# A pooled attention with a squared-ReLU network behind it, on one core: another order of the front, one key pair and three small steps moved

## The chip, the cores and the metric

The kernel runs on one core of a Trainium2 chip. The metric is the device time of one execution in microseconds. The core has a matrix engine (TensorE, "PE" in the profile), a vector engine (VectorE, "DVE"), an activation engine (ScalarE, "ACT"), a general engine (GpSimd, "POOL") and SyncE ("SP"), which here issues most of the transfers. Each engine has its own queue of instructions and works through it in order; engines wait for one another by semaphores.

## The reference

Eight batches of eight heads with 576 positions and 64 features per head; keys and values are averaged over groups of eight positions, which leaves 72 of each. The result of the attention, with the heads put side by side, is 4608 tokens of 512 features, and goes through a network of two weights with a squared ReLU between them. Everything is float32.

```python
k_p = k.reshape(B, H, Sp, 8, D).mean(axis=3)
v_p = v.reshape(B, H, Sp, 8, D).mean(axis=3)
scores = scale * np.matmul(q, k_p.transpose(0, 1, 3, 2))
scores = scores - np.max(scores, axis=-1, keepdims=True)
attn = np.exp(scores)
attn = attn / (np.sum(attn, axis=-1, keepdims=True) + 1e-09)
x = np.matmul(attn, v_p)           # -> (4608 tokens, 512), heads side by side
h = np.maximum(x @ w_in, 0.0)      # 512 -> 2048
out = h * h @ w_out                # 2048 -> 512
```

## The kernel before, in words

**Tiling.** The 4608 tokens go through in nine chunks of 512. A chunk has 16 steps, one for each block of 128 hidden features: a step computes one hidden block (`h_n`, products of the chunk's four tiles `x_0` to `x_3`, one for each pair of heads, with the first weights `wf_i`), and, three steps later (`LAG`), that block's share of the output (`o_0` to `o_3`, which stay in PSUM for the whole chunk). Step numbers in the code run on over the chunks: chunk 2's first step is 32. Between the two come the ReLU and the square on ScalarE (`r_n`). In the first two chunks (`PLAIN = 2`) the products are plain; from chunk 2 on the hidden blocks are made of seven products of halves instead of eight, from sums and differences of weights that VectorE and ScalarE prepare (`wf_i`, `w_S`) and of tokens, and the second product is split in a high and a low part (`gh`, `gl`).

**Attention.** It is made for the chunk ahead while the network of the current chunk runs. In chunks 0 and 1 a pair of heads goes through `token_scores` (products `sps` of queries `st` and keys `kf`, then on VectorE the two maxima `tm`, as minima of the negated scores, and on ScalarE eight exponentials `te`, four for each head), `token_normalise` (VectorE: a sum, a small product, a reciprocal, a product over all of `te`), `token_turn` (TensorE transposes into `pps`, copied to `sc`) and `weigh_values` (`av`, copied to `x_p`). From chunk 2 on the scores are transposed; `exponents` subtracts the maxima from `sc` on VectorE, takes exponentials on ScalarE and sums on GpSimd with an all-reduce over the partitions (`tot`, and `mx` for the maxima before it); `transpose_q` transposes the queries on VectorE (`qs`) and splits them in high and low parts `st` on ScalarE and VectorE. Keys and values of a batch are summed over their eight positions: batch 0's first three key pairs on VectorE (`reduce_k`, two reduces into `kq`), its fourth pair, its values, and batch 1's keys and values on GpSimd (`halve_k`, `halve_v`: three adds of halves each). TensorE turns the sums (`turn_k`, transposes into `kps`), ScalarE copies them to `kf`. `late_turn_k` is `turn_k` with its copy at once.

**Weights.** They are converted on the chip from their words: `magnitude` (ScalarE, two instructions for a weight tile) and `to_float32` (VectorE, three: a clamp and two combinations of bits). In the first chunk this is VectorE's main work.

**Products of zeros.** `keep_awake(c, t, n)` puts `n` products of a tile of zeros (`still`) in TensorE's queue, in chunk 0 only. `STIR` of them stand at the very start (`stir`), `STAY` behind the second pair's queries and keys (`stay`), and `AWAKE` ahead of each `token_scores`, `token_turn` and `weigh_values`.

**PSUM.** `o_0` to `o_3` have a buffer each; `h` has two; and the pool `ps_a` with the tag `a` has two, which `kps`, `pps` and, in chunk 1, `sps` go through in turn.

**What sets the order.** Every instruction is recorded through `InOrder` and stays in program order on its engine, so the listing of an engine is the order of the code; all of them have one line in the profile (L34). The front is written out by hand (lines 729 to 794). After it, `at(step, f, ...)` puts a function on a step, and the loop at the end goes through the steps. The functions in `on_pe` put their products between a step's hidden block and its output products; `late_turn_k` is not among these and runs behind the output products, at the head of the step's other work. `STEADY` and `EARLY` hold the steps of the attention's functions, relative to a pair's first step; the attention of chunk 3 (`PLAIN + 1`) begins beside chunk 1 and goes on in chunk 2's steps, 32 and up.

## Time and profile before

| | us |
|---|---|
| median of 3 runs (lowest, highest) | 910.28 (909.4, 911.02) |
| the profiled execution's own time | 910.27 |
| its span, from the first to the last instruction | 908.5 |
| TensorE busy | 894.3 (98%) |
| VectorE busy | 568.1 (63%) |
| ScalarE busy | 509.6 (56%) |
| GpSimd busy | 421.1 (46%) |

A row of a timeline reads: start in the span, duration, engine, line, operation, the tile written and the tiles read, the shapes, how many instructions it stands for, and in brackets the idle time ahead of it on this engine with what ended it. Where a row stands for several instructions, the duration is that of all together. Rows of TensorE have modelled ends, so neighbours may overlap a little. A list of waits gives the total, how many times and the longest. The granted clock of TensorE was 0.999 over this execution.

### The profile page before, as it was taken

What the parts mean: (1) busy time and instruction counts of PE and PEld (TensorE: products, weight loads), DVE (VectorE), ACT (ScalarE), POOL (GpSimd) and SP (SyncE); (2) the same over time, 40 slices, a digit from 0 to 9 for tenths busy, and PEclk for the clock granted to TensorE, in tenths of its full rate; (3) what the DMA queues carried; (4) which work ended last, traced back from release to release, by engine and by line L of the source; (5) the groups of instructions that cost most, each with busy time, mean ns of one, the idle gap of its engine ahead of it and who ended that gap; (6) DMA issues with size and microseconds to landing.
All of it is one profiled execution on the core that took longest, in us unless ns stands there. A gap on an engine that the chain in (4) does not pass through costs nothing.

```text
span 908.5 us, 14140 instructions
## 1 busy us (share of the span) xinstructions
PE 894.3 (98%) x5090; PEld 715.2 (79%) x5093; DVE 568.1 (63%) x946; ACT 509.6 (56%) x1017; POOL 421.1 (46%) x227
## 2 busy tenths in 40 slices
PE   8999999999999999999999999999999999999998
PEld 5444445777878888888888888888888888889987
DVE  7997778668688877456755575648544653353222
ACT  5866756656565656554655556455644564344442
POOL 3753245566555456566555655564444444200000
PEclk9999999999999999999999999999999999999999
DMA  9898574877555666665575556654533353245401
GB/s 222 263 261 189 140 177 110 229 227 196 130 155 141 143 143 142 178 156 118 133 207 135 120 143 179 153 132 117 170 109 113 105 164 116 96 173 197 175 1 47
DMA packets 157335, 138.72 MB, mean 153 GB/s; under 512 B 94488, under 2 KB 122136, under 8 KB 157264
## 3 DMA queue, kind: packets, MB, share of 16 engines
q1 hardware_dynamic: 128464, 127.13, 46.5%
q0 software_dynamic: 28800, 10.68, 10.3%
q8 instruction: 40, 0.66, 0.3%
q14 instruction: 31, 0.25, 0.1%
HBM read 119.65 MB, written 18.06 MB: 152 GB/s over the span
## 4 chain that ended last, share of the span: by engine, by line
PE 82%; DMA 6%; DVE 4%; ACT 2%; POOL 2%; issue 2%; SPq 1%; DVEq 0%; ACTq 0%; POOLq 0%
PE o L34 40%; PE h L34 35%; PE av L34 3%; PE sps L34 3%; SPq L34 1%; DMA rb<-rd 1%; POOL k L34 1%; DMA k<-in_k_dram 1%; DMA v<-in_v_dram 1%; DMA w_o<-kept 1%; DVE gl L34 1%; DVE wf_i L34 1%; DMA rd<-rr 1%; ACT sc L34 0%; DVE xf L34 0%
## 5 line engine op out<-in xcount | busy, mean ns | idle before, releaser
L34 PE MATMUL o<-w_o,gh 128*128 128x512 f32 x1024 | 322.3, 396 | 2.0 <-DMA w_o<-kept 2.0
L34 POOL PARTITION_ALL_REDUCE tot<-sc x56 | 187.8, 3403 | 86.4 <-issue 86.4
L34 PEld LDWEIGHTS o<-w_o,gh 128*128 128x128 f32 x1024 | 184.3, 188 | 46.8 <-issue 6.6
L34 PE MATMUL o<-w_o,gl 128*128 128x512 f32 x512 | 200.9, 392 | 0.0
L34 ACT ACTIVATE r<-h 128x512 f32<-128x512 f32 x144 | 83.6, 595 | 94.4 <-PE h L34 74.2
L34 PE MATMUL h<-x_T,w_S 128*128 128x256 f32 x1008 | 130.2, 283 | 0.5 <-ACT r L34 0.5
L34 POOL PARTITION_ALL_REDUCE mx<-sc x56 | 112.4, 2048 | 37.0 <-ACT sc L34 25.9
L34 PEld LDWEIGHTS h<-x_T,w_S 128*128 128x128 f32 x1008 | 124.9, 191 | 0.7 <-ACT r L34 0.7
L34 PEld LDWEIGHTS o<-w_o,gl 128*128 128x128 f32 x512 | 96.2, 188 | 21.3 <-DVE gl L34 0.4
L34 DVE TENSOR_TENSOR h<-h,u 128x256 f32<-128x256 f32 x168 | 72.6, 432 | 64.1 <-ACT u L34 33.7
L34 ACT COPY u<-h 128x256 f32<-128x256 f32 x112 | 41.8, 373 | 115.2 <-PE h L34 70.8
L34 PE MATMUL h<-x_B,w_A 128*128 128x256 f32 x672 | 98.6, 283 | 0.5 <-ACT r L34 0.5
L34 PEld LDWEIGHTS h<-x_B,w_A 128*128 128x128 f32 x672 | 91.6, 189 | 5.6 <-ACT r L34 1.1
L34 DVE TENSOR_TENSOR gl<-r,gh 128x512 fp32r<-128x512 f32 x128 | 92.1, 755 | 5.4 <-ACT gh L34 5.3
L34 POOL DMA_DIRECT2D k<-in_k_dram x36 | 44.1, 1225 | 109.1 <-issue 60.4
L34 POOL DMA_DIRECT2D v<-in_v_dram x36 | 44.1, 1224 | 107.4 <-issue 50.3
L34 DVE TENSOR_TENSOR u<-h,u 128x256 f32<-128x256 f32 x56 | 23.4, 417 | 101.9 <-ACT u L34 101.8
L34 ACT ACTIVATE r<-r 128x512 f32<-128x512 f32 x144 | 84.2, 625 | 1.1
L34 DVE TENSOR_TENSOR st<-qs,st 64x512 fp32r<-64x512 f32 x56 | 45.1, 806 | 61.8 <-ACT st L34 61.0
L34 ACT CAST gh<-r 128x512 fp32r<-128x512 f32 x128 | 78.9, 616 | 0.6 <-PE o L34 0.4
L34 ACT ACTIVATE sc<-sc 72x512 f32<-72x512 f32 x56 | 34.5, 632 | 69.3 <-DVE sc L34 69.3
L34 PE MATMUL h<-x,wf_i 128*128 128x512 f32 x128 | 57.8, 595 | 0.8 <-ACT x L34 0.8
(96 smaller groups left out, 1213.0 us busy)
## 6 DMA issues: line engine op xcount, KB each, us to landing
w_o<-kept SPq DMA_DIRECT2D x128, 512.0 KB
out_dram<-ob SPq DMA_DIRECT2D x36, 256.0 KB
raw_i<-in_moe_w_in_dram SPq DMA_DIRECT2D x16, 512.0 KB
raw_o<-in_moe_w_out_dram SPq DMA_DIRECT2D x16, 512.0 KB
kept<-w_o SPq DMA_DIRECT2D x16, 512.0 KB
rb<-rd SPq DMA_DIRECT2D x56, 128.0 KB
k<-in_k_dram POOLq DMA_DIRECT2D x36, 144.0 KB, 5.1
v<-in_v_dram POOLq DMA_DIRECT2D x36, 144.0 KB, 5.0
```

Of the source, the lines that this page charges most:

```text
L34: return lambda *a, **k: self.tc.keep_in_program_order(f(*a, **k))
```

## The change

1. **Fewer products of zeros.** `STAY` is 5 in place of 7 and `AWAKE` is (1, 1, 0) in place of (3, 2, 0): 2, 8 and 4 products less, 14 in all. The `stay` products now stand behind the second pair's scores and write to the pool `ps_a`.
2. **The third key pair of batch 0** is summed on GpSimd with three adds, no longer on VectorE with two reduces.
3. **The front in another order.** `token_scores` of chunk 0 gives its maxima and its exponentials as two functions, which the front calls apart. The normalisations and turns of pairs 0 and 1 come earlier. The second three conversions of the first weight tile, on VectorE, stand ahead of the normalisation of pair 3 (they stood behind it).
4. **Batch 1's keys.** `late_turn_k` takes a list of pairs: the first three stay in step 3, the fourth goes to step 4.
5. **Chunk 3.** `exponents` of its pair 1 and `transpose_q` of its pair 2 come one step later, 33 for 32.

TensorE, steps 3 to 5 of chunk 0, before (`kps`: transposes of batch 1's key sums; `sps_0`: scores of chunk 1's first pair; what stands in brackets are the engines whose semaphores the instruction waits for):

```order
L34 MATMUL o_3_565<-wf_o_463,r_0_468 128x512
L34 MATMUL kps_0_573<-ident,kq_172 128x72 [waits Pool_49] x4
L34 MATMUL h_4_601<-x_0_380,wf_i_0_471 128x512 [waits DVE_49,Activation_49]
...
L34 MATMUL sps_0_0_606<-kf_194,st_0_545 64x72 [waits DVE_49]
...
L34 MATMUL o_0_562<-wf_o_463,r_1_484 128x512 [waits DVE_49]
...
L34 MATMUL h_5_656<-x_0_380,wf_i_0_471 128x512
```

and with the change:

```order
L34 MATMUL o_3_552<-wf_o_450,r_0_455 128x512
L34 MATMUL kps_0_560<-ident,kq_173 128x72 [waits Pool_49] x3
L34 MATMUL h_4_587<-x_0_360,wf_i_0_458 128x512 [waits DVE_49,Activation_49]
...
L34 MATMUL sps_0_0_592<-kf_195,st_0_532 64x72 [waits DVE_49]
...
L34 MATMUL o_0_549<-wf_o_450,r_1_471 128x512 [waits DVE_49]
...
L34 MATMUL kps_3_625<-ident,kq_173 128x72 [waits DVE_49,Activation_49,Pool_49]
L34 MATMUL h_5_645<-x_0_360,wf_i_0_458 128x512
```

One of the four transposes moved from ahead of `h_4` to ahead of `h_5`, into a PSUM tile of its own, and there it waits for three engines.

VectorE, in the front, before (`tm_3`, `te_3`: pair 3's normalisation; `wf_i_0` with 256 columns: the first weight tile, in two parts):

```order
L34 TENSOR_TENSOR te_2_300<-te_2_300,tm_2_299 128x2x288
L34 TENSOR_SCALAR wf_i_0_343<-wf_i_0_343 128x256
L34 SCALAR_TENSOR_TENSOR wf_i_0_343<-wf_i_0_343,raw_i_0_0_85 128x256
L34 SCALAR_TENSOR_TENSOR wf_i_0_343<-raw_i_0_0_85,wf_i_0_343 128x256
L34 TENSOR_REDUCE tm_3_361<-te_3_362 128x8
L34 TENSOR_SCALAR tm_3_361<-tm_3_361 128x8
L34 RECIPROCAL tm_3_361<-tm_3_361 128x8
L34 TENSOR_TENSOR te_3_362<-te_3_362,tm_3_361 128x2x288
L34 TENSOR_SCALAR wf_i_0_343<-wf_i_0_343 128x256
```

and with the change:

```order
L34 TENSOR_TENSOR te_2_313<-te_2_313,tm_2_310 128x2x288
L34 TENSOR_SCALAR wf_i_0_350<-wf_i_0_350 128x256
L34 SCALAR_TENSOR_TENSOR wf_i_0_350<-wf_i_0_350,raw_i_0_0_85 128x256
L34 SCALAR_TENSOR_TENSOR wf_i_0_350<-raw_i_0_0_85,wf_i_0_350 128x256
L34 TENSOR_SCALAR wf_i_0_350<-wf_i_0_350 128x256
L34 SCALAR_TENSOR_TENSOR wf_i_0_350<-wf_i_0_350,raw_i_0_0_85 128x256
L34 SCALAR_TENSOR_TENSOR wf_i_0_350<-raw_i_0_0_85,wf_i_0_350 128x256
L34 TENSOR_REDUCE tm_3_344<-te_3_362 128x8
```

The second three conversions went ahead of the normalisation.

VectorE, the attention of chunk 3 beside chunk 2's first steps, before (`sc_1`: subtraction of the maxima; `qs_2`, `st_2`: queries of pair 2):

```order
L34 TENSOR_TENSOR gl_15_2283<-r_15_2218,gh_15_2282 128x512
L34 TENSOR_TENSOR sc_1_2151<-sc_1_2151,mx_1_0_2152 72x512
L34 TENSOR_TENSOR sc_1_2151<-sc_1_2151,mx_1_1_2153 72x512
L34 STREAM_TRANSPOSE qs_2_2311<-q_2_2032 128x512
L34 TENSOR_TENSOR st_2_2313<-qs_2_2311,st_2_2313 64x512 x2
L34 TENSOR_TENSOR wf_i_1_474<-wf_i_1_474,wf_i_0_471 128x4x128
L34 TENSOR_TENSOR w_S_2318<-wf_i_0_471,w_S_2318 128x512
L34 TENSOR_TENSOR xf_0_2339<-av_0_2340,rb_0_2290 128x512
```

and with the change:

```order
L34 TENSOR_TENSOR gl_15_2272<-r_15_2207,gh_15_2271 128x512
L34 TENSOR_TENSOR wf_i_1_461<-wf_i_1_461,wf_i_0_458 128x4x128
L34 TENSOR_TENSOR w_S_2292<-wf_i_0_458,w_S_2292 128x512
L34 TENSOR_TENSOR xf_0_2313<-av_0_2314,rb_0_2279 128x512
L34 TENSOR_TENSOR sc_1_2140<-sc_1_2140,mx_1_0_2141 72x512
L34 TENSOR_TENSOR sc_1_2140<-sc_1_2140,mx_1_1_2142 72x512
L34 STREAM_TRANSPOSE qs_2_2349<-q_2_2021 128x512
L34 TENSOR_TENSOR st_2_2351<-qs_2_2349,st_2_2351 64x512 x2
```

Four groups of the attention went behind the three rows that the network and the next tokens need.

The diff:

```diff
-    STIR, STAY, AWAKE = 10, 7, (3, 2, 0)
+    STIR, STAY, AWAKE = 10, 5, (1, 1, 0)
...
-    def late_turn_k(b):
-        turn_k(b)()
+    def late_turn_k(b, pairs=range(NPAIR)):
+        turn_k(b, pairs)()
...
-        def then():
+        def maxima():
             m = sb.tile([P, 3, 2, NTT], F32, name=f"tm_{c}_{p}", tag="tm", bufs=2)
-            e = w_tile(F32, f"te_{c}_{p}")[:, :, :NTT * SP_].rearrange("p i (t n) -> p i t n", t=NTT)
             for i in range(2):
                 DVE.tensor_reduce(m[:, 0, i], views[i], axis=AX.X, op=ALU.min)
+            live[c, p] = m
+
+        def exps():
+            m = live[c, p]
+            e = w_tile(F32, f"te_{c}_{p}")[:, :, :NTT * SP_].rearrange("p i (t n) -> p i t n", t=NTT)
             for i in range(2):
                 for t in range(NTT):
                     ACT.activation(e[:, i, t], views[i][:, t], AF.Exp, bias=m[:, 0, i, t:t + 1], scale=-1.0)
             live[c, p] = (e, m)
 
-        return then
+        def then():
+            maxima()
+            exps()
+
+        return (maxima, exps) if c == 0 else then
...
-    for p in range(3):
+    for p in range(2):
         reduce_k(0, p)
-    halve_k(0, 3)
+    for p in range(2, NPAIR):
+        halve_k(0, p)
...
-    exp = [token_scores(0, 0)]
+    tm[0], te[0] = token_scores(0, 0)
...
-    exp[0]()
-    keep_awake(0, ps_o.tile([P, 512], F32, name="stay", tag="o3"), STAY)
+    tm[0](), te[0]()
+    tm[1], te[1] = token_scores(0, 1)
+    tm[1](), te[1]()
+    keep_awake(0, ps_a.tile([P, 512], F32, name="stay", tag="a"), STAY)
     st[2] = turn_rows(0, 2)
-    exp.append(token_scores(0, 1))
+    token_normalise(0, 0)
     kf2 = turn_k(0, [2])
-    st[2](), kf2()
+    kf2(), st[2]()
+    sums = token_turn(0, 0)
     st[3] = turn_rows(0, 3)
...
     kf3 = turn_k(0, [3])
-    kf3()
...
+    tm[2], te[2] = token_scores(0, 2)
     sums()
     token_normalise(0, 1)
+    st[3](), kf3()
+    tm[2](), te[2]()
+    sums = token_turn(0, 1)
+    tm[3], te[3] = token_scores(0, 3)
+    tm[3]()
+    sums()
     magnitude(keys[0])
...
     token_normalise(0, 2)
     weigh_values(0, 0)()
+    te[3]()
     to_float32(keys[0], rows=slice(0, 1))
-    token_turn(0, 2)()
+    x1 = weigh_values(0, 1)
+    sums = token_turn(0, 2)
+    x1()
+    begin(0)
+    to_float32(keys[0], rows=slice(1, 2))
     token_normalise(0, 3)
-    to_float32(keys[0], rows=slice(1, 2))
-    weigh_values(0, 1)()
+    sums()
     magnitude(keys[1])
...
-    at(3, late_turn_k, 1)
+    at(3, late_turn_k, 1, range(NPAIR - 1))
+    at(4, late_turn_k, 1, [NPAIR - 1])
...
+    LATER = ((PLAIN + 1, 1, exponents), (PLAIN + 1, 2, transpose_q))
...
-                at(max(s + d, START[f]) if c == PLAIN and f in START else s + d - (f is transpose_q and (p != 2 if c >= PLAIN else p == 0)), f, c, p)
+                at(max(s + d, START[f]) if c == PLAIN and f in START else s + d - (f is transpose_q and (p != 2 if c >= PLAIN else p == 0)) + ((c, p, f) in LATER), f, c, p)
```

## The prediction

> **What bounds the kernel now.** I read the head of the page first, then the table by stage, then TensorE's waits, then the timelines around the edits.

> ```profile
> span 908.5 us, 14140 instructions
> PE 894.3 (98%) x5090; PEld 715.2 (79%) x5093; DVE 568.1 (63%) x946; ACT 509.6 (56%) x1017; POOL 421.1 (46%) x227
> 33.80:58.10 24.30, 23.50 (x75) 10.67 (x75) 24.06 (x27) 15.77 (x28) 22.49 (x19) 1.00 0.81 216
> 275.00:908.00 633.00, 628.64 (x3937) 551.90 (x3936) 348.43 (x616) 333.12 (x654) 278.92 (x130) 1.00 0.50 136
> ```

> The columns after a stretch are its length and the busy time of TensorE (PE), its weight loads, VectorE (DVE), ScalarE (ACT) and GpSimd (POOL). TensorE is busy 98% of the span; from 275 to 908 it is idle for 4.36 us in 633. So whatever delays TensorE once, early, is still there at the end: 4.36 us of idle spread over that time is not one place that can take it up. The exception to "TensorE alone" is the stretch 33.80 to 58.10, where VectorE is busy for 24.06 of 24.30 us. It converts weights there without a pause, and anything that comes to wait for VectorE waits for that whole queue. GpSimd is nearly as full, 22.49.

> ```profile
> PE sps L34 <- DVE xf L34: 1.5, 3, 0.9
> PE h L34 <- ACT r L34: 1.0, 2, 0.5
> PE kps L34 <- POOL kq L34: 0.8, 1, 0.8
> ```

> These are waits of TensorE (total, times, longest). The change touches all three: the key wait is one of 0.8, and of the other two, one each lies in chunk 3.

> **The change part by part.**

> *Fewer products of zeros.* Fourteen go.

> ```profile
> 1.45 4.45 PE L34 MATMUL stir<-still 128*128 128x512 bf16 x10 [1.45 <-DVE still L34]
> 10.10 1.68 PE L34 MATMUL stay<-still 128*128 128x512 bf16 x7
> 191.16 0.71 PE L34 MATMUL o<-w_o,gh 128*128 128x512 f32 x2 [1.69 <-DMA w_o<-kept]
> 191.94 0.62 PE L34 MATMUL o<-w_o,gh 128*128 128x512 f32 x2
> ```

> A product costs 1.68/7 = 0.24 us, so 14 × 0.24 = 3.4 us leave TensorE's queue before 34 us. I cost it at nothing, as the keys' load and VectorE set the pace there (below), and what is left over is hidden again by a later wait. The first ten products took 0.445 each, 0.205 more than the later ones: TensorE starts slow. A pause of 1.69 us (191.16) was followed by products of 0.355 where the next take 0.31. The products that go leave gaps nearer to that size, so I take no slowing in the front. [...]

> *Third keys on GpSimd, the front's new order.* Two kinds of row matter, VectorE's and GpSimd's:

> ```profile
> 10.93 1.95 DVE L34 TENSOR_REDUCE kq<-k 72x64 f32<-72x512 f32 x2 [1.06 <-DMA k<-in_k_dram]
> 20.82 0.82 DVE L34 TENSOR_REDUCE tm<-sps 128x4 f32<-128x288 f32 x2 [0.24 <-PE sps L34]
> 22.82 0.84 DVE L34 TENSOR_TENSOR te<-te,tm 128x576 f32<-128x576 f32 x1
> 23.59 1.35 DVE L34 TENSOR_SCALAR wf_i<-wf_i 128x256 f32<-128x256 f32 x1
> 25.91 0.56 DVE L34 SCALAR_TENSOR_TENSOR wf_i<-raw_i,wf_i 128x256 uint32<-128x256 uint32 x1
> 27.91 1.12 DVE L34 TENSOR_TENSOR te<-te,tm 128x576 f32<-128x576 f32 x1
> 28.96 0.54 DVE L34 TENSOR_SCALAR wf_i<-wf_i 128x256 f32<-128x256 f32 x1
> 30.00 0.43 DVE L34 SCALAR_TENSOR_TENSOR wf_i<-raw_i,wf_i 128x256 uint32<-128x256 uint32 x1
> ```
> ```profile
> 13.85 2.07 POOL L34 TENSOR_TENSOR k<-k 72x512 f32<-72x512 f32 x2 [13.41 <-DMA k<-in_k_dram]
> 16.00 0.45 POOL L34 TENSOR_TENSOR kq<-k 72x128 f32<-72x128 f32 x1
> 28.50 0.85 POOL L34 TENSOR_TENSOR vp<-v 72x128 f32<-72x128 f32 x1
> ```

> VectorE is rid of 1.95 us at 10.93. On GpSimd the same sum costs 2.07 + 0.45 = 2.52 us, and the data was there at 10.93, so it ends near 13.5, before the fourth pair's data (13.85). The fourth pair's sum therefore still ends at 16.45, and the scores that VectorE reads at 20.82 come from it. So VectorE's maxima of pair 3 start hardly earlier; I take 0.3. From there VectorE is short of time, and the order counts. The second three conversions (28.96 to 30.43: 1.46 us, clear of GpSimd, whose last add ends at 29.35) now stand ahead of the normalisation of pair 3, where the first three took 23.59 to 26.47, 2.88 us, under GpSimd's adds. They may so cost up to 1.42 more, and the normalisation, which now comes later, is spared some of it: its last product took 1.12 beside the adds and 0.84 earlier, and I take 0.5 for the whole of it. Net VectorE lateness: 1.42 − 0.5 − 0.3 = +0.6, taken as +0.7 with the rounding of starts; bounds −0.3 (nothing gets slower) and +2.0 (all three slowed, nothing spared, no earlier start, and half a microsecond for an add that starts just ahead of one). TensorE's own front may end as much as that later, but what follows hides it.

> *Batch 1's last key pair, step 3 to step 4.* This carries the forecast.

> ```profile
> 47.85 0.36 PE L34 MATMUL kps<-ident,kq 72*128 72x72 f32 x3
> 49.01 0.28 PE L34 MATMUL kps<-ident,kq 72*128 72x72 f32 x1 [0.80 <-POOL kq L34]
> 49.13 3.65 PE L34 MATMUL h<-x,wf_i 128*128 128x512 f32 x8
> 52.71 1.18 PE L34 MATMUL sps<-kf,st 64*64 64x72 f32 x20
> 53.82 3.70 PE L34 MATMUL o<-wf_o,r 128*128 128x512 f32 x8
> 57.36 3.60 PE L34 MATMUL h<-x,wf_i 128*128 128x512 f32 x8
> ```
> ```profile
> 56.87 1.28 DVE L34 SCALAR_TENSOR_TENSOR wf_i<-raw_i,wf_i 128x512 uint32<-128x512 uint32 x2
> 58.07 0.81 DVE L34 TENSOR_REDUCE tm<-sps 128x4 f32<-128x288 f32 x2
> 58.60 1.80 ACT L34 ACTIVATE te<-sps,tm 128x72 f32<-128x72 f32 x8 [6.60 <-issue]
> ```

> The 0.80 at 49.01 goes: the first three pairs' sums are ready. In its place the fourth transpose stands behind the output products (53.82) and ahead of the hidden block at 57.36. It needs a PSUM buffer from the pool of two whose buffers the scores at 52.71 have just taken (two tiles, one for each head of the pair). It can have the first of them only when four exponentials have read it, and the listing of the change gives it a wait on VectorE and ScalarE for that. Those exponentials wait for the maxima at 58.07, which stand behind VectorE's conversions. TensorE now comes there at 57.36 − 0.80 − 0.12 = 56.44 plus what the front is late. In the profile, four exponentials are done at 58.60 + 4 × 1.80/8 = 59.50; with VectorE 0.7 later, 60.20. The transpose takes 0.36/3 = 0.12 and the hidden block starts at 60.3 in place of 57.36: **+3.0 us**, bounds +2.0 and +4.3 by VectorE's bounds. The front's lateness and the 0.80 are inside this, not beside it. Behind the waiting transpose queues all of TensorE's work; VectorE and ScalarE have their own queues ready and lose nothing.

> *Chunk 3: one exponentials and one query split a step later.*

> ```profile
> 262.33 0.98 PE L34 MATMUL h<-x_B,w_A 128*128 128x256 f32 x6 [0.47 <-ACT r L34]
> 266.86 0.31 PE L34 MATMUL sps<-st,kl 128*72 128x192 f32 x1 [0.92 <-DVE xf L34]
> ```
> ```profile
> 257.94 1.28 DVE L34 TENSOR_TENSOR sc<-sc,mx 72x512 f32<-72x512 f32 x2
> 260.53 2.42 DVE L34 TENSOR_TENSOR st<-qs,st 64x512 fp32r<-64x512 f32 x2 [0.69 <-ACT st L34]
> 262.96 2.64 DVE L34 TENSOR_TENSOR wf_i<-wf_i,wf_i 128x512 f32<-128x512 f32 x1
> 266.13 0.68 DVE L34 TENSOR_TENSOR xf<-av,rb 128x512 f32<-128x512 f32 x1
> 259.45 6.59 POOL L34 PARTITION_ALL_REDUCE tot<-sc x2 [4.70 <-issue]
> ```

> VectorE's subtraction of maxima, transpose and split (257.94 to 262.95) now stand behind the sum for the next weights and the product at 266.13, so TensorE's 0.92 can go; and ScalarE reaches its squares without the exponentials and casts ahead of them, so the 0.47 can go. The all-reduce at 259.45 starts when the exponentials are done, so 2 to 2.5 us later, and beside it one VectorE row took 2.64 where the same kind takes 0.68 elsewhere; this slowing now meets the split and the next chunk's sums. The split is late next, and the scores that read it can then wait. Bounds 0 and −1.39; I take half, **−0.7**.

> Sum: +3.0 − 0.7 = +2.3. The profiled run took 910.27 for a span of 908.50 (1.77 around it), and the median is 910.28: 910.27 + 2.3 = **912.6**.

> **The rivals.** *B, no difference.* The conversions ahead of 58.07 run beside GpSimd's adds for batch 1. If these overlap less than before, VectorE comes to the maxima about 1 us earlier than I take, and chunk 3 gives its larger half: +2.2 − 1.0 = +1.2, 911.5. For it: the stretch is the most crowded one, and 2.4 us would suffice for the whole loss. Against: neither the loads nor the adds of batch 1 are touched.

> *C, slower still.* An idle time of 3 us on TensorE is longer than any in this profile after its start. If the array starts slow again, ten products at 0.205 more cost 2.05: 912.6 + 2.0 = 914.6. [...]

> *D, not slower.* The maxima come before TensorE does. The transpose is free if four exponentials are done by 56.44, that is if VectorE starts the maxima by 56.44 − 1.43 = 55.0, 3.1 us earlier than now (1.43 is 59.50 − 58.07). Then 0.80 and up to 1.39 are saved: 910.27 − 2.2 = 908.1. For it: VectorE's 1.95 us and 3.4 us of zeros are really gone, and the front's chain is shorter in operations. Against: 24.06 of 24.30 busy from 33.80 on, and a start at 20.82 that hangs on a load and on GpSimd.

> **How the numbers follow.** Forecast 0.55, B 0.23, C 0.13, D 0.09. The range takes the forecast's own bounds, +2.0 − 1.39 = +0.6 and +4.3, so 910.9 to 914.6, and is opened by 0.2 and 0.3 for C and B: 910.7 to 914.9. What a measurement can tell from no change is 0.2%, 1.8 us. Faster: D, 0.09. Within 0.2%: B and the part of the forecast under +1.8, about a fifth of it, 0.23 + 0.11 = 0.34. Slower: the rest, 0.57.

> **What would show it.** The key step is right if TensorE's row for one transpose of keys near 57 us has an idle of 2 to 4 us ahead of it, put down to ScalarE's exponentials (or to GpSimd's sum, which ended long before), and if the next hidden block starts near 60.3. The maxima at 58.07 should start near 58.8. It is wrong if that transpose has no idle (D) or one under 1.5 us (B), or if the hidden products right behind it take more than their 0.45 each (C). The front is right if the second three conversions take over 1.46 us and the wait of 0.80 is gone; wrong if the maxima of pair 3 start well before 20.5. Chunk 3 is right if the waits of 0.47 and 0.92 are gone and others of about half their sum come up within three steps.

## The result, and the profile after

The changed kernel is slower: a median of 915.45 us over 4 runs (913.97 to 916.49) against 910.19 over 4 runs of the kernel before; the ratio is 1.0056 with a 95% interval of 1.0039 to 1.0074, some 5.2 us. The forecast had the sign and the place but not the size: 912.6, with a range that ended at 914.9. The profiled execution after took 916.49, the slowest of the four, for a span of 914.7 (before 908.5), so the traces show 6.2 us where the medians show 5.2.

The table by stage of the changed kernel, with the same columns as before:

```profile
20.80:33.80 13.00, 9.87 (x41) 3.63 (x41) 11.02 (x19) 7.69 (x23) 7.30 (x9) 0.75 0.99 318
33.80:58.10 24.30, 24.30 (x80) 11.01 (x78) 21.15 (x24) 19.11 (x34) 20.40 (x19) 0.93 0.81 212
275.00:908.00 633.00, 631.48 (x3955) 554.32 (x3955) 353.41 (x621) 337.28 (x662) 281.59 (x133) 1.00 0.50 137
```

The first of these stretches in the kernel before:

```profile
20.80:33.80 13.00, 12.13 (x53) 5.16 (x54) 12.45 (x23) 10.41 (x25) 8.08 (x9) 1.00 0.99 329
```

The last three numbers of a row are TensorE's granted clock, the busy share of the DMA engines and the GB/s that they moved. The clock was 1.00 in these three stretches before; now it is 0.75 and 0.93 in the two that hold the end of the front. VectorE, busy for 24.06 us between 33.80 and 58.10 before, now has pauses there (21.15).

TensorE's timeline of the changed kernel, from the end of the front to step 5:

```profile
23.93 0.39 PE L34 MATMUL pps<-still 128*128 128x512 bf16 x1
25.58 1.07 PE L34 MATMUL pps<-ident,te 128*72 128x128 f32 x8 [1.25 <-DVE te L34]
28.41 3.75 PE L34 MATMUL h<-x,wf_i 128*128 128x512 f32 x4 [1.76 <-DVE wf_i L34]
32.09 1.97 PE L34 MATMUL av<-sc,vp 72*64 72x512 f32 x4
34.40 1.91 PE L34 MATMUL pps<-ident,te 128*72 128x128 f32 x8
39.58 10.66 PE L34 MATMUL h<-x,wf_i 128*128 128x512 f32 x24
53.52 0.36 PE L34 MATMUL kps<-ident,kq 72*128 72x72 f32 x3
58.39 3.70 PE L34 MATMUL o<-wf_o,r 128*128 128x512 f32 x8
62.60 0.25 PE L34 MATMUL kps<-ident,kq 72*128 72x72 f32 x1 [0.50 <-ACT te L34]
62.69 3.65 PE L34 MATMUL h<-x,wf_i 128*128 128x512 f32 x8
```

Three rows of the kernel before, two of TensorE and one of VectorE:

```profile
26.62 1.96 PE L34 MATMUL h<-x,wf_i 128*128 128x512 f32 x4 [0.82 <-ACT x L34]
33.92 10.66 PE L34 MATMUL h<-x,wf_i 128*128 128x512 f32 x24
32.18 0.68 DVE L34 COPY sc<-pps 72x512 f32<-72x512 f32 x1
```

Four hidden products take 3.75 us at 28.41 (1.96 before; they start 1.79 later, behind a wait for VectorE's converted weights), eight transposes 1.91 at 34.40 (1.07 at 25.58). The block of 24 hidden products starts at 39.58, 5.66 later than before (33.92). The old wait of 0.80 for GpSimd's sum is gone at 53.52. The fourth transpose waits 0.50, put down to ScalarE's exponentials, and the hidden block behind it starts at 62.69: 5.33 later than before (57.36). That is already the whole of the difference of the medians.

The clock in two narrow stretches of the same execution, and the 3.41 us ahead of its fall:

```profile
23.78:27.19 3.41, 1.61 (x11) 0.90 (x9) 3.24 (x5) 3.41 (x12) 3.17 (x5) 1.00 1.04 387
27.00:28.00 1.00, 0.00 (x0) 0.00 (x0) 0.96 (x2) 1.00 (x3) 0.90 (x2) 0.59 0.89 348
37.00:38.00 1.00, 1.00 (x3) 0.49 (x2) 0.52 (x3) 1.00 (x3) 0.89 (x2) 0.79 0.81 188
```

It fell to 0.50 at 27.2 and came back at 37.4, 10.2 us later.

VectorE, GpSimd and ScalarE, the rows that answer to the prediction's:

```profile
21.83 0.82 DVE L34 TENSOR_REDUCE tm<-sps 128x4 f32<-128x288 f32 x2 [1.63 <-PE sps L34]
28.18 0.54 DVE L34 TENSOR_SCALAR wf_i<-wf_i 128x256 f32<-128x256 f32 x1
29.22 0.42 DVE L34 SCALAR_TENSOR_TENSOR wf_i<-raw_i,wf_i 128x256 uint32<-128x256 uint32 x1
36.35 0.69 DVE L34 COPY sc<-pps 72x512 f32<-72x512 f32 x1 [2.96 <-PE pps L34]
61.06 0.81 DVE L34 TENSOR_REDUCE tm<-sps 128x4 f32<-128x288 f32 x2
```
```profile
14.56 2.26 POOL L34 TENSOR_TENSOR k<-k 72x512 f32<-72x512 f32 x2 [0.72 <-DMA k<-in_k_dram]
16.90 0.85 POOL L34 TENSOR_TENSOR kq<-k 72x128 f32<-72x128 f32 x1
61.54 1.80 ACT L34 ACTIVATE te<-sps,tm 128x72 f32<-128x72 f32 x8 [5.01 <-DVE tm L34]
```

The maxima of pair 3 start at 21.83, 1.01 later than before; the copy of pair 3's turned exponentials, the last thing that VectorE does for the front, waits 2.96 us for TensorE (the transposes at 34.40) and starts at 36.35 in place of 32.18; and chunk 1's first maxima start at 61.06 in place of 58.07, 3.0 us late.

In chunk 3:

```profile
269.99 0.31 PE L34 MATMUL sps<-st,kl 128*72 128x192 f32 x1 [0.35 <-DVE st L34]
274.79 0.95 PE L34 MATMUL h<-x_B,w_S 128*128 128x256 f32 x6 [0.53 <-DVE h L34]
268.24 2.41 DVE L34 TENSOR_TENSOR st<-qs,st 64x512 fp32r<-64x512 f32 x2 [0.69 <-ACT st L34]
270.68 2.62 DVE L34 TENSOR_TENSOR wf_i<-wf_i 128x512 f32<-128x512 f32 x1
```

The waits of 0.47 and 0.92 are gone. In their place TensorE waits 0.35 for the split (268.24) and 0.53 for a difference of halves that stands behind a weight row of 2.62, which took 0.67 in the kernel before (266.73).

### The profile page after: what moved, and what is told of

It reads as the page before. It is cut to its first block, busy times and chain, and to the rows that moved or that the text cites. A ratio compares the mean times of both kernels' runs of the same rounds, so it can differ in the third digit from the quotient of the medians.

```text
span 914.7 us, 14117 instructions
## 1 busy us (share of the span) xinstructions
PE 897.0 (98%) x5078; PEld 715.1 (78%) x5079; DVE 563.6 (62%) x944; ACT 510.3 (56%) x1018; POOL 418.8 (46%) x230
## 4 chain that ended last, share of the span: by engine, by line
PE 80%; DVE 7%; DMA 6%; issue 2%; ACT 2%; SPq 1%; POOL 1%; DVEq 0%; POOLq 0%; ACTq 0%
PE o L34 39%; PE h L34 35%; PE av L34 3%; PE sps L34 3%; DMA v<-in_v_dram 2%; DMA w_o<-kept 2%; SPq L34 1%; DMA k<-in_k_dram 1%; DVE wf_i L34 1%; DVE gl L34 1%; DVE xf L34 1%; DMA q<-in_q_dram 1%; POOL k L34 1%; DMA rb<-rd 1%; DVE vp L34 0%
## 5 line engine op out<-in xcount | busy, mean ns | idle before, releaser
L34 PE MATMUL o<-w_o,gh 128*128 128x512 f32 x1024 | 322.5, 396 | 2.0 <-DMA w_o<-kept 2.0
L34 POOL PARTITION_ALL_REDUCE tot<-sc x56 | 186.7, 3382 | 91.6 <-issue 91.5
L34 PEld LDWEIGHTS o<-w_o,gh 128*128 128x128 f32 x1024 | 184.3, 188 | 47.2 <-issue 7.0
L34 PE MATMUL o<-w_o,gl 128*128 128x512 f32 x512 | 201.1, 393 | 0.0
L34 ACT ACTIVATE r<-h 128x512 f32<-128x512 f32 x144 | 83.6, 595 | 94.2 <-PE h L34 72.2
L34 PE MATMUL h<-x_T,w_S 128*128 128x256 f32 x1008 | 130.6, 283 | 1.0 <-ACT r L34 0.4
L34 POOL PARTITION_ALL_REDUCE mx<-sc x56 | 110.5, 2019 | 36.2 <-ACT sc L34 26.4
L34 PEld LDWEIGHTS h<-x_T,w_S 128*128 128x128 f32 x1008 | 124.9, 191 | 1.6 <-ACT r L34 0.6
L34 PEld LDWEIGHTS o<-w_o,gl 128*128 128x128 f32 x512 | 96.2, 188 | 21.7 <-DVE gl L34 0.8
L34 DVE TENSOR_TENSOR h<-h,u 128x256 f32<-128x256 f32 x168 | 72.7, 433 | 62.3 <-ACT u L34 33.2
L34 ACT COPY u<-h 128x256 f32<-128x256 f32 x112 | 41.7, 372 | 118.5 <-PE h L34 70.3
L34 PE MATMUL h<-x_B,w_A 128*128 128x256 f32 x672 | 98.5, 282 | 0.0
L34 PEld LDWEIGHTS h<-x_B,w_A 128*128 128x128 f32 x672 | 91.8, 189 | 4.8
L34 POOL DMA_DIRECT2D v<-in_v_dram x36 | 44.0, 1222 | 111.4 <-issue 50.3
L34 DVE TENSOR_TENSOR gl<-r,gh 128x512 fp32r<-128x512 f32 x128 | 91.5, 751 | 5.4 <-ACT gh L34 5.3
L34 POOL DMA_DIRECT2D k<-in_k_dram x36 | 44.1, 1225 | 108.4 <-issue 61.5
L34 DVE TENSOR_TENSOR u<-h,u 128x256 f32<-128x256 f32 x56 | 23.4, 418 | 102.7 <-ACT u L34 102.6
L34 ACT ACTIVATE r<-r 128x512 f32<-128x512 f32 x144 | 84.2, 625 | 1.1
L34 DVE TENSOR_TENSOR st<-qs,st 64x512 fp32r<-64x512 f32 x56 | 44.5, 795 | 62.7 <-ACT st L34 61.8
L34 ACT CAST gh<-r 128x512 fp32r<-128x512 f32 x128 | 78.9, 617 | 0.6 <-PE o L34 0.4
L34 ACT ACTIVATE sc<-sc 72x512 f32<-72x512 f32 x56 | 34.5, 632 | 68.1 <-DVE sc L34 68.1
L34 PE MATMUL h<-x,wf_i 128*128 128x512 f32 x128 | 60.3, 616 | 1.8 <-DVE wf_i L34 1.8
```

Of the source, the lines that this page charges most:

```text
L34: return lambda *a, **k: self.tc.keep_in_program_order(f(*a, **k))
```

## The experiments

Where a ratio is given, the time is a median of 7 to 12 runs, and the kernel before, run beside them on the same chip, had medians of 910.3 to 911.2 (907.3 to 918.0 in single runs); the others are one execution. A ratio's interval is 0.16 to 0.3% to each side, 1.4 to 2.7 us, so the profiles carry most of what follows. A ratio need not equal the quotient of the two medians.

Each execution also has its mean granted clock on record. One stretch of 3.4 us at half clock takes 0.002 off this mean (0.998 in the profile with only the keys moved, which has one such stretch, from 59.7). Every profile has one more fall behind the last product, worth 0.001 at most. So I say that an execution kept its clock where the mean is 0.999 or 1.000.

### The parts alone, in the kernel before

**Only the fourth key pair in step 4.**

```diff
-    at(3, late_turn_k, 1)
+    at(3, late_turn_k, 1, range(NPAIR - 1))
+    at(4, late_turn_k, 1, [NPAIR - 1])
```

> The kernel before with only batch 1's fourth key pair put from step 3 to step 4. The predicted mechanism (the transpose waits for a PSUM buffer until four exponentials of chunk 1's first pair are done, and these wait for VectorE's conversions): idle of 2.5 to 3.5 us ahead of the single transpose, the next hidden block starts near 60.0 in place of 57.36, and the time is 912.3 to 913.0 (+2 to +2.8). Rival (VectorE reaches the maxima sooner than 58, or the loss is taken back by later waits): 909.5 to 910.8, no idle over 1 us at the transpose.

Measured: 913.93, ratio 1.0019 (0.9989 to 1.0049). The medians differ by 3.2 us, but the interval of the ratio holds no change as well, so the time alone doesn't show the loss. Its timelines of VectorE and TensorE:

```profile
58.33 0.81 DVE L34 TENSOR_REDUCE tm<-sps 128x4 f32<-128x288 f32 x2
59.91 0.36 PE L34 MATMUL kps<-ident,kq 72*128 72x72 f32 x1 [3.22 <-ACT te L34]
60.06 5.16 PE L34 MATMUL h<-x,wf_i 128*128 128x512 f32 x8
```

The mechanism is there, at the size that was worked out: 3.22 us of idle, the next hidden block at 60.06 (expected near 60.0). And behind it is what the prediction had as rival C: the eight products take 5.16 in place of 3.60, since the clock was at 0.50 from 59.7 to 63.1. Matched product by product with the kernel before, TensorE is 2.7 late at the start of this block and 4.3 at its end. Of these 4.3 us, 2.1 are taken back later (4.3 to 3.4 at 191, where the kernel before waits 1.69 for its weights, then to 2.2 at the end). Two of the ten executions kept their clock, and took 912.68 and 913.62.

**Only fewer products of zeros.**

```diff
-    STIR, STAY, AWAKE = 10, 7, (3, 2, 0)
+    STIR, STAY, AWAKE = 10, 5, (1, 1, 0)
```

> The kernel before with the change's number of zero products (5; 1, 1, 0) and nothing else. The forecast's term: nothing, 910.2 to 911.2, since no stretch without products gets near 3 us. Rival (these products hold the clock in the front): the granted clock falls to 0.50 for some microseconds between 12 and 34, and the time is 912 to 914.

Measured: 911.07, ratio 1.0002 (0.9984 to 1.0020). In the profiled execution the clock fell, from 14.7 to 21.5; the block of 24 products started 1.25 later (35.17). The kernel before had cover for a part of it: the wait of 0.80 for GpSimd at 49 shrank to 0.34, and of the 0.8 us that were left, 0.5 remained by 250 (0.9 at the end). Five of the ten executions kept their clock, against 68 of 95 of the kernel before. So both sides of the expectation are half right: the clock can fall here, but that it falls oftener than in the kernel before isn't shown by ten executions, and no loss is seen in the time.

**Only chunk 3's two functions a step later.**

```diff
-... s + d - (f is transpose_q and (p != 2 if c >= PLAIN else p == 0)), f, c, p)
+... s + d - (f is transpose_q and (p != 2 if c >= PLAIN else p == 0)) + ((c, p, f) in LATER), f, c, p)
```

> The kernel before with only chunk 3's two functions put one step later. The forecast's term: -0.7 us, 909.5. The changed kernel's trace, matched product by product with the one before, shows 1.1 us gained between 262 and 267 and 1.0 lost again by 273 (a split waited for, and a subtraction of halves slowed to 2.62 beside the all-reduce): by that 910.2, within 0.5. Rival (the gain whole, -1.39): 908.8.

Measured: 911.68, ratio 1.0010 (0.9984 to 1.0037): no difference seen. Against the kernel before, TensorE's lead in this execution was 0.85 at 216 us, 1.94 at 267, 1.24 at 270 and 0.9 at 301: 1.1 gained, and 1.0 lost again behind it.

### What the clock does, in the changed kernel

**The old number of zero products.**

```diff
-    STIR, STAY, AWAKE = 10, 5, (1, 1, 0)
+    STIR, STAY, AWAKE = 10, 7, (3, 2, 0)
```

> The changed kernel with the old number of zero products (7; 3, 2, 0), at their new places. After the change TensorE's granted clock is 0.50 from 27.4 to 37.8 us, and from the end of a product of zeros at 24.3 until 28.41 TensorE runs nothing but eight transposes. Theory A (transposes do not hold the clock, a stretch of about 3.1 us without real products drops it): the added products stand ahead of the transposes and wait no longer than these, so the last one ends near 24.5 and the stretch without products stays near 3.9 us; the clock still falls, and the time stays at 915.4, within 1. Theory B (the number of zero products alone holds the clock): granted clock 1.00 all through, 2.5 to 3.5 us faster than the changed kernel, 912 to 913.

Measured: 915.29, ratio 1.0055 (1.0030 to 1.0081), as theory A said; but the clock did not fall where it said. It fell at 19.9, behind pair 0's turn, pair 3's query turn and a wait of 1.29 for GpSimd, and came back at 23.3. The old number of products in the new order did not hold it in every execution: five of the ten kept it. These five took 914.38 to 918.9 and the other five 914.29 to 917.68, so in this run the time did not follow the clock.

**Three zero products behind pair 2's turn.**

```diff
     x1()
+    keep_awake(0, ps_o.tile([P, 512], F32, name="stay2", tag="o3"), 3)
     begin(0)
```

> The changed kernel with three zero products more, placed directly behind pair 2's transposes and ahead of the first hidden products, where TensorE waits 1.76 us. Theory A (transposes do not hold the clock): products then run at about 26.6 to 27.4, no stretch without products is longer than 2.3 us, the granted clock stays at 1.00 from 20.8 to 58.1, the hidden products from 28.41 take 1.96 for four and not 3.75, and the block of 24 products that started at 39.58 starts at about 36.5; time 912 to 913. Theory C (the clock is not the cause; VectorE and the loads are late and set the pace): the clock may be mended, but the block of 24 still starts after 39 and the time stays at 915 to 916.

Measured: 914.20, ratio 1.0038 (1.0012 to 1.0063).

```profile
28.78 1.98 PE L34 MATMUL h<-x,wf_i 128*128 128x512 f32 x4 [1.04 <-DVE wf_i L34]
35.63 10.66 PE L34 MATMUL h<-x,wf_i 128*128 128x512 f32 x24
61.47 0.25 PE L34 MATMUL kps<-ident,kq 72*128 72x72 f32 x1 [1.82 <-ACT te L34]
59.94 0.81 DVE L34 TENSOR_REDUCE tm<-sps 128x4 f32<-128x288 f32 x2
```

The clock is mended at this place: the four products take 1.98, and the block of 24 starts at 35.63, 4 us earlier than in the changed kernel. But of these 4 us only 1.1 are left at the hidden block of step 5 (61.56 for 62.69). The transpose waits 1.82 in place of 0.50: VectorE's maxima start at 59.94, and TensorE's gain runs into them. The median is not that of a kernel at full clock: nine of the ten executions have a mean of 0.994 to 0.998, and in the profiled one TensorE ran slowly earlier, before 17 us (see the last section).

**Transposes in place of these zero products.**

```diff
+    for t in range(8):
+        PE.transpose(more[:, t % 4 * P:(t % 4 + 1) * P], ident, ident)
     begin(0)
```

> The changed kernel with eight transposes of the identity where the earlier run had three zero products, behind pair 2's turn (about 0.9 us of TensorE's time). Theory A (transposes do not hold the clock): the granted clock is 0.50 at some point between 24 and 38 as in the changed kernel, though TensorE is busy at 26.6 to 27.5. Theory B (any work holds it): it stays at 1.00 from 24 to 38. An execution whose clock falls earlier in the front tells nothing of this.

One run, 917.23. The clock is in the third number from the end:

```profile
22.01:25.42 3.41, 2.05 (x10) 0.38 (x7) 3.31 (x7) 3.41 (x12) 3.17 (x5) 1.00 1.05 362
25.42:28.83 3.41, 3.41 (x17) 3.25 (x18) 3.25 (x5) 2.99 (x7) 2.76 (x4) 0.52 0.86 335
28.83:32.24 3.41, 3.41 (x13) 1.22 (x13) 3.18 (x8) 0.53 (x2) 0.00 (x0) 0.98 0.96 301
```

It fell at 25.55, before the eight added transposes ran (26.89), and it came back at 28.96, after 3.4 us in which TensorE did sixteen transposes on end and next to nothing else. The sign that the expectation gave for theory A, a clock of 0.50 between 24 and 38, did come, but the fall came too early to test the added work. What the execution does show is that the clock came back over transposes, which speaks against theory A in the form that they do not count. It is one execution.

### Both causes taken away

**The clock held:** the old number of zero products and seven more, four behind pair 3's query turn and three behind pair 2's turn.

```diff
     st[3] = turn_rows(0, 3)
+    keep_awake(0, ps_o.tile([P, 512], F32, name="stay3", tag="o3"), 4)
...
     x1()
+    keep_awake(0, ps_o.tile([P, 512], F32, name="stay2", tag="o3"), 3)
     begin(0)
```

> The changed kernel with the old number of zero products and seven more at the two places where its front has TensorE do transposes and waits alone: four behind pair 3's query turn, three behind pair 2's turn. All profiles of the new front so far show a stretch of half clock between 8 and 38 us, each at another place. Theory (clock and waiting transpose are both needed to explain +5): no half clock; VectorE comes to chunk 1's first maxima about 0.7 late as forecast, 58.8 in place of 60 to 62; the hidden block behind the fourth transpose starts at 60.4; 912 to 913.2. Rival (the new order itself is slow for VectorE, clock or not): maxima at 60 or later, 914 to 915.5.

Measured: 914.19, ratio 1.0037 (1.0010 to 1.0065); the profiled execution took 913.28.

```profile
58.74 0.81 DVE L34 TENSOR_REDUCE tm<-sps 128x4 f32<-128x288 f32 x2
60.33 0.25 PE L34 MATMUL kps<-ident,kq 72*128 72x72 f32 x1 [1.43 <-ACT te L34]
60.42 3.65 PE L34 MATMUL h<-x,wf_i 128*128 128x512 f32 x8
```

With a clock of 1.00 all through the front, VectorE is 0.67 late at the maxima (forecast 0.7) and the hidden block starts at 60.42 (forecast 60.3). The agreement of 0.67 and 0.7 is in part luck. At the copy of pair 3's turned exponentials VectorE was 1.24 late (33.42 for 32.18); from there to the maxima, where it converts weights beside GpSimd's adds, it took 25.32 us. This stretch took 25.74 to 25.89 in the six profiles with the old front, and 24.71 to 26.82 in the eleven with the new one.

The median is above what was expected, and it is not that of a held clock: three of the eight executions kept it (913.28, 913.70 and 914.68), and the other five have a median of 915.70.

**The same, and all keys in step 3.**

```diff
-    at(3, late_turn_k, 1, range(NPAIR - 1))
-    at(4, late_turn_k, 1, [NPAIR - 1])
+    at(3, late_turn_k, 1)
```

> The same, and all four key pairs of batch 1 turned in step 3 again. Theory: neither the clock nor the transpose is left, the time is that of the kernel before within 1 us: 909.3 to 911.3. Rival (the new order itself is slow for VectorE): 912 to 914, with TensorE waiting for converted output weights at about 55.

Measured: 912.92, ratio 1.0026 (1.0011 to 1.0042): neither theory's whole, nearer to the rival. All ten executions kept their clock.

```profile
58.70 3.60 PE L34 MATMUL h<-x,wf_i 128*128 128x512 f32 x8
59.73 0.81 DVE L34 TENSOR_REDUCE tm<-sps 128x4 f32<-128x288 f32 x2
```

The hidden block of step 5 starts at 58.70, 1.34 later than before, and VectorE's maxima at 59.73, 1.66 later. So in this execution the new front is slower by more than a microsecond also with the clock up and the keys in their old place.

**Only the keys back in step 3**, zero products as in the change.

> The changed kernel with all four of batch 1's key pairs turned in step 3 again. Theory V (the fourth transpose waits for exponentials that wait for VectorE; in five profiles the hidden block behind it starts 1.62 to 1.73 us after VectorE starts the maxima of chunk 1's first pair): without it TensorE waits only where its own front is late or where converted weights are; 913.2 to 914.7 (0.7 to 2 faster than the changed kernel's 915.4), most where the clock stays up. Rival (TensorE's own late front, +5.7 at 34 us, sets everything): 915.0 to 916, as the wait of the transpose was only 0.50 in the profiled execution.

Measured: 914.69, ratio 1.0036 (1.0011 to 1.0060), as theory V said. In the profiled execution (917.31) it was the rival that ruled: the clock fell twice, from 11.3 to 18.1 and from 28.3 to 38.6, the block of 24 started at 40.55, and nothing waited behind it. Which of the two limits decides changes from one execution to the next. The two executions that kept their clock took 910.10 and 911.65, as the kernel before does; the other seven, with means of 0.990 to 0.996, have a median of 915.33.

### Which part of the front's order

**The scores of pair 2 ahead of the turn of the fourth keys.**

> The changed kernel with the scores of pair 2 put ahead of the turn of the fourth keys, in batch 0's front. In the changed kernel this turn waits for GpSimd's sum until 17.80, and VectorE then idles 1.94 and 1.63 us ahead of the maxima of pairs 2 and 3, which start at 19.38 and 21.83 (before: 17.62 and 20.82). Theory V (this idle time is the lateness that VectorE carries to the maxima of chunk 1, +3.0 us at 61.06): the maxima of pair 2 start near 17.4, those of pair 3 near 20.7, chunk 1's first near 59.7, and the time is 913.4 to 914.7. Rival (when the loads land decides): no idle is saved beyond 0.5, 915 to 916.

Measured: 917.38, ratio 1.0083 (1.0058 to 1.0108), the wrong way. The maxima of pair 2 started at 20.16, not at 17.4: the clock had fallen at 8.6 and stayed down to 15.4, fell again from 29.1 to 32.5, and a third time at 63.2, in a wait of 3.28 for the exponentials. It tells nothing of the order.

**The third keys on VectorE again.**

> The changed kernel with the third key pair summed on VectorE again. Theory V' (the third pair on GpSimd delays the fourth pair's sum: 17.75 against 16.45): the fourth sum ends near 16.5, the maxima of pair 3 start near 20.8, and the time is 914 to 915, up to 1.4 faster. Rival (the 1.95 us are missed on VectorE, which now normalises pairs 0 and 1 early): the first normalisation starts 1.5 to 2 us later and the time is 915.4 to 916.5.

Measured: 916.96, ratio 1.0063 (1.0042 to 1.0085). The fourth sum ended earlier, at 15.8, but the first normalisation started 1.7 later (14.52 for 12.85), as the rival said. TensorE now waited 3.33 us for pair 0's normalised exponentials, the clock was down from 17.5 to 24.4, and the maxima of pair 3 started at 25.11. Nothing is gained by it.

**The clock held, the keys back, and the scores of pairs 2 and 3 ahead of the turns of pairs 0 and 1.**

```diff
     st[3] = turn_rows(0, 3)
     keep_awake(...)
+    tm[2], te[2] = token_scores(0, 2)
+    tm[2]()
+    sums = token_turn(0, 0)
+    sums()
     kf3 = turn_k(0, [3])
...
+    tm[3], te[3] = token_scores(0, 3)
+    tm[3]()
+    sums = token_turn(0, 1)
```

> The changed kernel with the clock held and the keys in step 3 (912.9 before this), and in the front the scores of pairs 2 and 3 ahead of the turns of pairs 0 and 1 on TensorE. Theory (the turns wait for normalised exponentials and hold up the scores that VectorE's last maxima need: these started at 19.82 and 22.92, in the kernel before at 17.62 and 20.82): they start near 17.9 and 20.9, the block of 24 hidden products near 34.3, time 909.5 to 911.5. Rival (the third keys on GpSimd or the moved conversions cost it): maxima earlier but the time within 0.7 of 912.9.

Measured: 913.61, ratio 1.0016 (0.9996 to 1.0037). The maxima started at 18.67 and 22.53, only 1.15 and 0.39 earlier than without this step, after a wait of 1.39 for the queries of pair 3; TensorE was 1.2 late at step 4 (1.3 without this step). The theory isn't borne out.

### Second profiles, and a version from the findings

**The changed kernel again.**

> The changed kernel once more, for a second profile. Theory: half clock for a multiple of 3.4 us somewhere in the front, at another place than 27.2 to 37.4, and whichever place it is, the hidden block behind the fourth transpose starts 1.6 to 1.75 us after VectorE starts chunk 1's first maxima, unless TensorE itself comes later. Rival: another rule.

One run, 918.59. The clock was down from 11.2 to 14.6 and from 24.9 to 31.7.

```profile
34.08 0.69 DVE L34 COPY sc<-pps 72x512 f32<-72x512 f32 x1 [0.99 <-PE pps L34]
60.87 0.81 DVE L34 TENSOR_REDUCE tm<-sps 128x4 f32<-128x288 f32 x2
62.40 0.25 PE L34 MATMUL kps<-ident,kq 72*128 72x72 f32 x1 [1.38 <-ACT te L34]
62.49 3.65 PE L34 MATMUL h<-x,wf_i 128*128 128x512 f32 x8
```

Another place of the clock, the same end: the hidden block 1.62 behind the start of the maxima. But VectorE's copy waits only 0.99 us for TensorE, and not 2.96, and comes 1.9 late (34.08 for 32.18).

**The kernel before again.**

> The kernel before once more, for a second profile: the fourth key pair's data at 12.5 to 14.5 us, chunk 1's first maxima at 57 to 59, granted clock 1.00 from 5 us on or one stretch of half clock of 3.4 us. Chunk 0's block behind the second output products starts within 1 us of 57.4.

One run, 909.44: the clock at 1.00 throughout, the maxima at 57.62, the hidden block of step 5 at 56.92. So two profiles of the kernel before lie 0.45 apart at these places.

**The kernel before with the fourth keys turned ahead of the scores of step 4**, four zero products more, and chunk 3's functions a step later.

> A version from the findings: the kernel before, with batch 1's fourth key pair turned in step 4 ahead of the scores (where it waits for no exponentials), four zero products more in the front, and chunk 3's two functions a step later. If what was found holds: the wait of 0.80 for GpSimd's sum is gone but about 0.45 comes back, as the scores wait for the copy of the fourth keys; the clock falls in fewer executions; 909 to 910.3, within 0.2% of the kernel before. If zero products cost as much as they hold: 910.3 to 912.

Measured: 914.63, ratio 1.0035 (1.0011 to 1.0059), and so slower than the kernel before. The front was ahead (the block of 24 at 32.93, a whole microsecond earlier), but then:

```profile
52.91 1.17 PE L34 MATMUL sps<-kf,st 64*64 64x72 f32 x18 [1.88 <-ACT kf L34]
54.02 5.40 PE L34 MATMUL o<-wf_o,r 128*128 128x512 f32 x8
```

The third score product, the first that reads batch 1's keys, waits 1.88, and not 0.45, for ScalarE to copy the fourth of them, and the clock falls again, so that eight products take 5.40 in place of 3.70. Its twelve executions lie between 905.46 and 920.30; the six that kept their clock have a median of 913.1. None of the variants is shown to beat the kernel before.

## Why the prediction was right or wrong

**The waiting transpose: right.** In the eight profiles in which this transpose stands in step 4 and waits, the hidden block starts 1.62 to 1.74 us after VectorE starts the maxima (among them the kernel before with the keys moved 60.06 − 58.33; changed kernel 62.69 − 61.06 and 62.49 − 60.87; clock held 60.42 − 58.74). The prediction had 60.3 − 58.77 = 1.5. Its +3.0 and 60.3 were measured as +2.7 and 60.06 where only this was changed, and as +3.06 and 60.42 in the changed kernel with the clock held.

**The term that was mis-sized: VectorE's lateness at these maxima, +0.7, at most +2.0.** It measured +3.0 (61.06) and +2.8 (60.87 in the second profile). In two executions of the new front at full clock it was +0.67 and, with the keys back, +1.66: inside the bounds, and at the size taken only once. The two profiles of the changed kernel, whose clock was down in the front, have 1.1 to 2.3 us more, and this is the step that the prediction costed at nothing: "The products that go leave gaps nearer to that size, so I take no slowing in the front." It looked at the gaps one by one, of which none in the changed kernel's front is over 1.8 us. But in the 3.41 us ahead of the fall TensorE was busy for 1.61 in all (23.78:27.19 above): a gap of 1.25 and the first 0.54 of one of 1.76 lie in them.

In the first profile the chain can be followed. The clock is at half for 10.2 us, and TensorE's last transposes of the front come late. VectorE, 1.1 late until then (its last conversion ahead of the wait starts at 32.70 for 31.57), is idle for 2.96 us ahead of its copy and so 4.2 late at 36.35. Its queue of conversions, with the maxima at the end, gives 1.2 of it back, and it is 3.0 late at 61.06. In the second profile the copy comes 1.9 late, and the conversions add 0.9. So the same lateness came about in two ways, and how much of it is the clock's is known for neither. The sum with the measured term is +5.3 at step 5, outside the +4.3 that the prediction took for its upper bound.

**The front's lateness is hidden behind the transpose: right, and for that reason so much of it does not show.** TensorE's front was 5.66 late in the changed kernel and 1.7 in the run with three products behind pair 2's turn; step 5 was 5.33 and 4.2 late. Mending TensorE's clock late in the front gave 4 us, of which 1.1 got through: two limits stand side by side there. The medians are too coarse for this. That run, 914.20, the keys put back, 914.69, and both causes away, 912.92, lie 0.8 to 2.5 us below 915.45, and each ratio is uncertain by about 2.

**What the clock of the single executions adds.** Of 95 executions of the kernel before, 68 kept their clock and have a median of 910.0; the other 27 have 912.9. So that kernel loses its clock too, only less often. With the new front and the keys back, two of nine kept it, and were 5.2 and 3.7 us below the median of the rest; with 21 zero products more, ten of ten kept it. So with the keys in step 3 the new order kept its clock with these products and mostly lost it without them. With only the keys moved, two of ten kept it, and still took 912.68 and 913.62: the key pair costs some 3 us by itself, and in the profile the wait that it brings was followed by a fall. The changed kernel has both. One of its five executions kept its clock and took 915.49, no less than the others (913.97 to 918.59). These are few executions each, and no trace of that one was kept.

**Rival C: right as a mechanism, too narrow in its place and chance.** It expected TensorE to run slow again only behind the 3 us of idle ahead of the transpose. It did so there when only the keys were moved (5.16 for 3.60, 1.6 us, forecast 2.0); in the changed kernel TensorE comes there so late that hardly a wait is left, and the clock had already fallen in the front. The chance of 0.13 looks too low: with only the keys moved, eight of ten executions lost their clock. Rivals B and D did not come, since VectorE reached the maxima late and not early.

**The conversions ahead of pair 3's normalisation: wrong, and it didn't matter.** Forecast up to 1.42 dearer; the three moved rows took 0.54 to 0.42 each (28.18 to 29.64, 1.46 in all), as before. The lateness at this place came from "VectorE's maxima of pair 3 start hardly earlier; I take 0.3": they start 1.01 later. GpSimd's fourth sum ended at 17.75 for 16.45, as its data landed later (14.56 for 13.85) and its last add took 0.85 for 0.45. The turn that waits for it starts only 0.3 later (17.80 for 17.50), but the scores of pair 2 now stand behind this turn and ahead of those of pair 3.

**Chunk 3: −0.7 forecast, near nothing measured.** What was gained (1.1) was lost within 10 us to the split and the row of 2.62, which the prediction had named as late next.

**"4.36 us of idle spread over that time is not one place that can take it up": too strong, and misread.** Of the 4.36 us, 3.3 lie behind the last product, which ends at 904.68; 1.0 is left. And yet in the execution with only the keys moved, 2.1 of 4.3 us were taken back behind step 5, the first 0.9 of it by 191, where the kernel before waits for weights, and the rest behind 275.

**What stays open.** With the clock held and the keys in step 3, the new front still costs 0.26% (0.11 to 0.42%), of which the profile shows 1.3 us at step 5. It holds seven zero products more than the kernel before (seven took 1.68 us there, at 10.10), the third keys on GpSimd and the new order, and the run with the scores ahead of the turns did not tell these apart. The two executions without the additional products that kept their clock, 910.10 and 911.65, speak for these products as the cost, but two are too few to show it. Why the changed kernel took 915.49 with its clock kept is open too. A part of the rest lies in waits for the kept output weights between 280 and 560 us, 0.3 us in the kernel before and up to 3.0 in the run with the scores ahead:

```profile
PE o L34 <- DMA w_o<-kept: 0.3, 1, 0.3
```
```profile
PE o L34 <- DMA w_o<-kept: 3.0, 3, 1.6
```

They differ between two executions of one kernel (0.6 and 2.8 in the changed kernel, where TensorE's lateness went from 4.95 at 290 to 6.2 at 550 in the first profile), and no run here was made to separate them.

## What to carry to other kernels

A moved instruction takes its buffer's history with it: before moving a transpose, look up who last read the buffer that it will get, and how long that reader's own queue is. Where two limits end at the same place, taking away either one shows little; take both away in one run before calling a cause small, and sort the executions by their clock before comparing medians. And before removing work that seems to do nothing, add up how busy the engine is over every few microseconds, not only how long its longest pause is (here 1.61 of the 3.41 us ahead of a fall, with no pause over 1.8).

## What was not expected of the hardware

**The clock fell behind stretches that were not idle.** Fifteen falls were found in the first 70 us of ten profiles. In the 3.41 us ahead of each, TensorE was busy for 0.42 to 2.4 us; the emptiest and the fullest of these stretches, in the kernel before with only the keys moved and in the second profile of the changed kernel, beside the emptiest such stretch between 5 and 70 us of the profile before, which had no fall:

```profile
56.28:59.69 3.41, 0.42 (x1) 0.00 (x0) 3.41 (x8) 0.83 (x5) 1.23 (x1) 1.00 0.91 259
```
```profile
21.45:24.86 3.41, 2.40 (x9) 0.41 (x9) 3.28 (x6) 3.41 (x11) 3.17 (x5) 1.00 1.04 342
```
```profile
8.50:11.91 3.41, 2.42 (x12) 1.13 (x12) 2.35 (x4) 0.76 (x2) 0.00 (x0) 1.00 1.01 190
```

**Half clock lasted 3.4, 6.8 or 10.2 us.** These were the lengths of all the recorded stretches ahead of the last product. In the changed kernel TensorE was busy without a pause from 28.41 on, so for all of the 3.41 us from 30.60 to 34.01, and the clock came back only at 37.4; in the run with transposes for zero products it was back after 3.4 us of transposes. What brought it back isn't settled here.

**In one run the clock and the durations disagree.** In the run with three zero products behind pair 2's turn the clock reads 1.00 throughout, and yet sixteen score products took 1.99 us at 12.32, 1.8 times the 1.11 elsewhere. At a recorded clock of 0.50, eight transposes took 1.91 (34.40 in the changed kernel) where they take 1.07 at 1.00, 1.8 times too. That TensorE was at half clock there is my estimate from these two ratios; the record doesn't show it.
